# Gate loop and feed-forward kernel: rows of w3 and w_out fetched as one tile, four at a time, and a two-word conversion with one three-operand instruction fewer

## The chip, the cores and the metric

The kernel runs on one core of a Trainium2 chip. The metric is device time in microseconds, the median over executions; lower is better. Each run executed the kernel before on the same chip in alternation. A ratio is the mean time of one kernel's fast runs over the mean of the other's of the same rounds, so it is not quite the ratio of the medians that are quoted.

In the tables of the profile PE is TensorE (PEld its weight loads), DVE is VectorE, ACT is ScalarE, POOL is GpSimd, and SPq is the queue of SyncE, which issues all transfers here.

## The reference

```python
B, H, S, D = 4, 8, 768, 48
scale = np.minimum(mag, 0.999) / (mag + 1e-06)        # mag = |a_re + i a_im|
for t in range(S):                                    # complex recurrence, decay by the gate
    S_re, S_im = (ar * S_re - ai * S_im + kv), (ar * S_im + ai * S_re)
    y[:, :, t] = np.einsum('bhd,bhde->bhe', q[:, :, t], S_re)
# ... then, on x = y as (3072, 384):
a = x @ w1; b = x @ w2                                # 384 x 1024 each
h = a * b @ w3                                        # 1024 x 1024
return h @ w_out                                      # 1024 x 384
```

The four weight matrices arrive as 64-bit floats. The core has no such type, so the kernel reads them as pairs of 32-bit words and puts 32-bit floats together from them: it shifts the high word left by three, puts its top two bits (the sign and one of the exponent; "the sign" below) back, and adds the top three bits of the low word, rounded ("the carry" below). Since h is linear in w3, it multiplies w3 by w_out once and uses the product.

## The kernel before

The first stage does two things side by side. It takes w3 and w_out row by row (eight rows of 128 by 1024 and 128 by 384), converts them, and multiplies them into eight sums. And it computes the gates of the first unit (half of the 768 time steps of one batch entry; there are eight units), a chain that alternates between ScalarE and VectorE. Each piece of weights takes one of three raw buffers:

```python
    def convert(dst, src, halves):
        r, m = dst.shape[1:]
        raw = cv["raw"].tile([P, r, m, 2], I32, tag="raw", name="raw")          # pool of 3
        nc.sync.dma_start(out=raw.rearrange("p r m w -> p r (m w)"), in_=src)
        lo, hi = raw[:, :, :, 0], raw[:, :, :, 1]
        low = cv["low"].tile([P, r, m], I32, tag="low", name="low")
        b = dst.bitcast(I32)
        if halves:          # w3: carry into the low half of each word, sign into the high half
            ...             # two ScalarE instructions
            nc.vector.tensor_scalar(out=b, in0=hi, scalar1=3, scalar2=None, op0=OP.logical_shift_left)
        else:               # w_out, w1, w2
            nc.scalar.activation(out=low, in_=lo.bitcast(U32), func=AF.Copy, scale=2.0 ** -29)
            nc.vector.tensor_scalar(out=b, in0=hi, scalar1=3, scalar2=0x3FFFFFFF, ...)
            nc.vector.scalar_tensor_tensor(out=b, in0=hi, scalar=-0x40000000, in1=b, ...)
        nc.vector.tensor_tensor(out=b, in0=b, in1=low, op=OP.add)
```
```python
        row_work(0, 4)                       # row 0 in four parts
        load_gates(0)
        take_qk(0)
        steps = gates(0, True)
        for f in range(KF):                  # KF = 8 rows
            if f:
                row_work(f)                  # loads and converts row f
            if f == 2:
                load_qkv(0)
            if f >= KF - 2:
                continue
            for j in range(KF):
                fuse(f, j)                   # line 924, the product on TensorE
            for _ in range(2):
                next(steps, None)            # two steps of the gates
```

KL and QL, the tiles into which K and Q are moved at the end of the gates, stand empty until then.

Of the kernel before, what the change touches and what calls it, by code (L numbers as in the profile page):

```python
# [10 lines left out]
FP = mybir.dt.float32  # L11
I32 = mybir.dt.int32
U32 = mybir.dt.uint32
U16 = mybir.dt.uint16
BF = mybir.dt.bfloat16
AF = mybir.ActivationFunctionType
OP = mybir.AluOpType
# [357 lines left out]
def kernel(  # L375
# [36 lines left out]
    nc = tc.nc  # L412
    B, H, D, S = qt.shape
    P = 128
# [3 lines left out]
    FF = w1.shape[1]  # L418
    KD = DM // P
    DG = P // H  # L420
    KF = FF // P
    WB = 2 * P
# [13 lines left out]
    w1s = weights_pool.tile([P, FF // WB, KD, WB], FP, name="w1s")  # L436
    w2s = weights_pool.tile([P, FF // WB, KD, WB], FP, name="w2s")
# [7 lines left out]
    one = fast.enter_context(tc.tile_pool(name="one", bufs=1))  # L445
# [36 lines left out]
    def load_rows(dst, src, u, which=range(KD), queue=nc.sync):  # L482
        b, h = divmod(u, 2)
        for i, f in enumerate(which):
            queue.dma_start(out=dst[:, i, 0:TT], in_=src[b, :, DG * f:DG * (f + 1), h * TT:(h + 1) * TT].rearrange(
                "h d s -> d h s"))

    def load_gates(u):
        g = g_t.setdefault(u, {})
        for n, src in (("re", art), ("im", ait)):  # L490
            g[n] = one.tile([P, KD, TT], FP, tag=n, name=n)
            load_rows(g[n], src, u)

    def take_qk(u):
        g = g_t.setdefault(u, {})
        g["q"] = gate_pool[u % 2].tile([P, KD, TT], FP, tag="q", name="q")
        g["k"] = gate_pool[u % 2].tile([P, KD, TT + 1], FP, tag="k", name="k")

    def load_qkv(u):
        b, h = divmod(u, 2)  # L500
        if "q" not in g_t.get(u, {}):
            take_qk(u)
        g = g_t[u]
        load_rows(g["k"], kt, u)
        load_rows(g["q"], qt, u)


        vr = one.tile([P, UC, DM], FP, tag="vr", name="vr")
        nc.sync.dma_start(out=vr, in_=v[b, h * TT:(h + 1) * TT].rearrange("(c p) e -> p c e", p=C))
        g["vr"] = vr  # L510
# [306 lines left out]

    cv = {}

    def convert(dst, src, halves):  # L820
        r, m = dst.shape[1:]
        raw = cv["raw"].tile([P, r, m, 2], I32, tag="raw", name="raw")
        nc.sync.dma_start(out=raw.rearrange("p r m w -> p r (m w)"), in_=src)
        lo, hi = raw[:, :, :, 0], raw[:, :, :, 1]
        low = cv["low"].tile([P, r, m], I32, tag="low", name="low")
        b = dst.bitcast(I32)
        if halves:
            ends = low.rearrange("p r m -> p (r m)")
            nc.scalar.activation(out=ends.bitcast(U16)[:, 0::2].rearrange("p (r m) -> p r m", r=r), in_=lo.bitcast(U32),
                                 func=AF.Copy, scale=2.0 ** -29)  # L830
            nc.scalar.activation(out=ends.bitcast(BF)[:, 1::2].rearrange("p (r m) -> p r m", r=r), in_=hi.bitcast(FP),
                                 func=AF.Sign)
            nc.vector.tensor_scalar(out=b, in0=hi, scalar1=3, scalar2=None, op0=OP.logical_shift_left)
        else:
            nc.scalar.activation(out=low, in_=lo.bitcast(U32), func=AF.Copy, scale=2.0 ** -29)
            nc.vector.tensor_scalar(out=b, in0=hi, scalar1=3, scalar2=0x3FFFFFFF, op0=OP.logical_shift_left,
                                    op1=OP.bitwise_and)
            nc.vector.scalar_tensor_tensor(out=b, in0=hi, scalar=-0x40000000, in1=b, op0=OP.bitwise_and,
                                           op1=OP.bitwise_or)
        nc.vector.tensor_tensor(out=b, in0=b, in1=low, op=OP.add)  # L840

    def load_weight(dst, src, halves=False):
        if src.dtype == FP:
            nc.sync.dma_start(out=dst, in_=src)
        else:
            convert(dst, src, halves)

    def words(src):
        return (src if src.dtype == FP else src.bitcast(I32)).rearrange("(i p) m -> p i m", p=P)
# [34 lines left out]
    w3_t = {}  # L884

    def rounding():

        stack = ExitStack()
        for n, k in (("raw", 3), ("low", 2)):
            cv[n] = stack.enter_context(tc.tile_pool(name=n, bufs=k))  # L890
        return stack

    def columns(src, j0, j1):
        n = 1 if src.dtype == FP else 2
        return words(src)[:, :, n * j0:n * j1]

    def w12_work():
        return [lambda d=d, w=w, n=n: load_weight(d[:, n], columns(w, n * WB, (n + 1) * WB))
                for n in range(FF // WB) for d, w in ((w1s, w1), (w2s, w2))]

    def row_work(f, parts=1):

        if f == 0:
            w3_t["wo"] = one.tile([P, KF, DM], FP, tag="ab", name="wo_s")
        w3_t[f] = two.tile([P, FF], FP, tag="xT", name="w3s")

        def some(n):
            step = FF // parts
            load_weight(w3_t[f][:, n * step:(n + 1) * step].rearrange("p (i m) -> p i m", i=1),
                        columns(w3t, n * step, (n + 1) * step)[:, f:f + 1], True)  # L910
        some(0)
        load_weight(w3_t["wo"][:, f:f + 1], words(wo)[:, f:f + 1])
        for n in range(1, parts):
            some(n)


    sums = []
# [51 lines left out]
    def ffn(u, parts=1):  # L969
        if u == 0:  # L970
            return [lambda j=j: ffn_ab(u, j) for j in range(KF)] + [p for t in range(UC) for p in ffn_out(u, t, parts)]
        last = ffn_out(u, UC - 1)[0]
        return [lambda j=j: ffn_ab(u, j) for j in range(KF)] + [lambda: (out_sums(u), last())] + out_pair(u)
# [17 lines left out]
    with tc.manual_schedule(engines={mybir.EngineType.PE}):  # L991

        phase = rounding()
        row_work(0, 4)
        load_gates(0)
        take_qk(0)
        steps = gates(0, True)
        for f in range(KF):
            if f:
                row_work(f)  # L1000
            if f == 2:
                load_qkv(0)
            if f >= KF - 2:
                continue
            for j in range(KF):
                fuse(f, j)
            for _ in range(2):
                next(steps, None)
        work = w12_work()
        for f in work[:2]:  # L1010
            f()
        for _ in steps:
            pass
        for f in range(KF - 2, KF):
            for j in range(KF // 2):
                fuse(f, j)
        fill = [lambda f=f, j=j: [fuse(f, j + x) for x in range(2)] for f in range(KF - 2, KF) for j in range(KF // 2, KF, 2)]
        load_gates(1)
        steps = gates(1, False)
        take_qk(1)  # L1020
        rest = ffn(0, 2)
        work = work[2:]
        for i, p in enumerate(pieces(0)):
            for f in p:
                f()
            if i in (1, 3, 6, 9):
                fill.pop(0)()
            if i == 0:
                for f in work[:2]:
                    f()  # L1030
                load_qkv(1)
            if i >= 2:
                next(steps)
            if i in (5, 7):
                work[2 + (i == 7)]()
        for i, f in enumerate(rest[:HEAD]):
            f()
            if i < 2:
                work[4 + i]()
            if i == 2:  # L1040
                phase.close()
            if i < 6:
                next(steps)
            if i == KF - 1:
                for _ in steps:
                    pass
        late = fast.enter_context(tc.tile_pool(name="late", bufs=1))
        look = check_weights(fast.enter_context(tc.tile_pool(name="looks", bufs=2)))
        out_weights()
        for u in range(1, NU):  # L1050
            steps = gates(u + 1, False) if u + 1 < NU else iter(())
            unit(u, steps, rest[HEAD:] if u == 1 else ffn(u - 1), look if u > 1 else iter(()), AHEAD[u])
            for _ in steps:
                pass
        for _ in look:
            pass
        judge()
        for f in ffn(NU - 1):
            f()
# [41 lines left out]
```

## Time and profile before

| | before |
|---|---|
| median of the time | 581.5 us (579.2 to 582.9) |
| span of the profiled execution | 581.6 us |
| TensorE idle | 34.8 us, of it 18.4 waiting for converted rows |
| row 7 ready for TensorE | 60.64 us |
| first feed-forward matmul | 89.12 us |

Read it so: TensorE is busy for 94 per cent of the span, so nearly all that can be won lies in its idle time. Idle time on other engines matters only where TensorE waits for them. The lines that show the waits are in the prediction.

### The profile page before, as it was taken

The numbers are of one execution on the slowest core, as the hardware profiler recorded it, in microseconds if no ns is written. First come the engines' busy times: TensorE is split into PE (matmuls) and PEld (weight loads), VectorE is DVE, ScalarE is ACT, GpSimd is POOL, SyncE is SP. The second block draws the span as 40 slices with busy tenths as digits, with TensorE's granted clock in tenths as the row PEclk, the third lists the DMA queues.
The fourth block names the chain that finished last, engine by engine and source line by source line (L and its number), as shares of the span: only waits on it lengthen the run. The fifth ranks groups of instructions, "written<-read, shape, count | busy, mean of one in ns | idle before, by whom it ended". The sixth has DMA issues, their size and how long they took to land.

```text
span 581.6 us, 9282 instructions
## 1 busy us (share of the span) xinstructions
PE 546.8 (94%) x3682; PEld 388.0 (67%) x3682; DVE 341.3 (59%) x507; ACT 348.5 (60%) x576; POOL 3.5 (1%) x9
## 2 busy tenths in 40 slices
PE   4579898999999999999989999999989999999995
PEld 2345585567656885679556975687557966697564
DVE  6898588965771477535952677444852787241121
ACT  5898648464764589628973799459973945111100
POOL 2000000000000000000000000000000000000000
PEclk9779999999999999999999999999999999999999
DMA  7877999376056335973486336935484103300001
GB/s 233 278 289 274 228 308 300 105 156 170 26 157 146 96 106 178 244 194 116 140 229 162 112 121 189 240 97 162 127 188 117 57 27 87 89 3 29 0 4 43
DMA packets 46340, 84.74 MB, mean 146 GB/s; under 512 B 4688, under 2 KB 36176, under 8 KB 45392
## 3 DMA queue, kind: packets, MB, share of 16 engines
q1 hardware_dynamic: 46288, 84.06, 51.1%
q8 instruction: 31, 0.51, 0.4%
q14 instruction: 21, 0.17, 0.1%
HBM read 60.42 MB, written 4.72 MB: 112 GB/s over the span
## 4 chain that ended last, share of the span: by engine, by line
PE 64%; ACT 13%; DMA 11%; DVE 8%; issue 3%; SPq 0%; ACTq 0%; DVEq 0%
PE m L723 34%; PE p L768 9%; PE o L803 7%; DMA raw<-in_w_dram 5%; PE kv L703 4%; PE sc L665 4%; PE y L692 3%; DMA look<-in_w_dram 3%; PE tp L653 2%; DMA vr<-in_v_dram 2%; ACT gZ L544 2%; ACT gR L544 2%; ACT re L544 1%; DVE gA L576 1%; DVE gZ L600 1%
## 5 line engine op out<-in xcount | busy, mean ns | idle before, releaser
L723 PE MATMUL m<-xT,w1s 128*128 128x384 f32 x384 | 135.4, 489 | 5.5 <-ACT xT L694 3.1
L723 PE MATMUL m<-xT,w2s 128*128 128x384 f32 x384 | 134.3, 486 | 0.0
L723 PEld LDWEIGHTS m<-xT,w2s 128*128 128x128 f32 x384 | 73.0, 190 | 50.9
L723 PEld LDWEIGHTS m<-xT,w1s 128*128 128x128 f32 x384 | 71.0, 190 | 51.8 <-ACT xT L694 4.3
L729 DVE TENSOR_TENSOR ab<-m,a 128x384 f32<-128x384 f32 x64 | 35.5, 556 | 82.7 <-PE m L723 74.4
L924 PE MATMUL f<-wo_s,w3s 128*128 128x384 f32 x128 | 51.0, 559 | 18.4 <-DVE wo_s L840 18.4
L728 ACT COPY a<-m 128x384 f32<-128x384 f32 x64 | 30.4, 476 | 49.7 <-PE m L723 49.6
L655 ACT COPY KT<-tp 128x384 f32<-128x384 f32 x40 | 33.7, 853 | 35.3 <-PE tp L653 35.2
L803 PE MATMUL o<-w3o,ab 128*128 128x384 f32 x160 | 53.8, 487 | 0.0
L924 PEld LDWEIGHTS f<-wo_s,w3s 128*128 128x128 f32 x128 | 27.5, 220 | 39.4 <-DVE wo_s L840 20.3
L665 PE MATMUL sc<-QL,KL 96*128 96x128 f32 x384 | 47.2, 276 | 1.9 <-DMA QL<-q 1.4
L665 PEld LDWEIGHTS sc<-QL,KL 96*128 96x128 f32 x384 | 45.7, 192 | 3.0 <-DMA QL<-q 1.5
L803 PEld LDWEIGHTS o<-w3o,ab 128*128 128x128 f32 x160 | 29.6, 190 | 18.9 <-issue 0.4
L692 PE MATMUL y<-A,V 128*32 128x128 f32 x768 | 39.3, 275 | 0.0
L667 DVE COPY_PREDICATED A<-causal,sc 128x512 f32<-128x512 int32 x48 | 34.0, 738 | 5.8 <-PE sc L665 5.5
L710 DVE TENSOR_TENSOR T<-kv,T 96x512 f32<-96x512 f32 x16 | 11.0, 687 | 42.4 <-PE kv L703 42.4
L692 PEld LDWEIGHTS y<-A,V 128*32 128x32 f32 x768 | 32.9, 109 | 3.6 <-issue 1.4
L692 PE MATMUL y<-QL,T 96*32 96x128 f32 x640 | 34.6, 272 | 0.0
L768 PE MATMUL p<-To,So 128*128 128x192 f32 x168 | 31.5, 331 | 0.5 <-DVE U L756 0.5
L544 ACT ACTIVATE re<-gZ 128x1152 int32<-128x1152 f32 (+3 forms) x20 | 19.2, 970 | 20.8 <-DVE gZ L600 16.4
L692 PEld LDWEIGHTS y<-QL,T 96*32 96x32 f32 x640 | 31.3, 110 | 0.0
L703 PE MATMUL kv<-V,KT 128*96 128x64 f32 x320 | 30.0, 246 | 0.9 <-ACT KT L655 0.9
(116 smaller groups left out, 760.8 us busy)
## 6 DMA issues: line engine op xcount, KB each, us to landing
look<-in_w_dram SPq DMA_DIRECT2D x28, 512.0 KB, 4.0
raw<-in_w_dram SPq DMA_DIRECT2D x7, 1024.0 KB, 8.0
raw<-in_w_dram SPq DMA_DIRECT2D x8, 768.0 KB, 7.0
KL<-gR SPq DMA_DIRECT2D x24, 192.5 KB, 3.4
KL<-k SPq DMA_DIRECT2D x24, 192.5 KB, 4.2
re<-in_a_re_dram SPq DMA_DIRECT2D x24, 192.0 KB, 5.4
im<-in_a_im_dram SPq DMA_DIRECT2D x24, 192.0 KB, 3.3
k<-in_k_dram SPq DMA_DIRECT2D x24, 192.0 KB, 3.7
```

What stands on the lines that cost most here:

```text
L544: chain(nc.scalar.activation(**kw))
L655: nc.scalar.copy(out=KT_t[u, c][:, :, :, x].rearrange("p h d f -> p f d h"), in_=tp.rearrange("p f (d h) -> p f d h", h=H))
L665: nc.tensor.matmul(out=sc[:, j], lhsT=KL[:, x * n + j, w], rhs=QL[:, x * n + j, w], start=True, stop=True)
L667: nc.vector.copy_predicated(out=A[:, x * n:(x + 1) * n], data=sc, mask=causal.rearrange("p (h t) -> p h t", h=1).to_broadcast([P, n, C]))
L692: nc.tensor.matmul(out=o, lhsT=a, rhs=b, start=s0, stop=s1)
L703: nc.tensor.matmul(out=kv[:, hd], lhsT=KT[:, hd].rearrange("p d x f -> p (d x f)"), rhs=V[:, hd], start=True, stop=True)
L723: nc.tensor.matmul(out=m, lhsT=w[:, j * P // WB, f, j * P % WB:j * P % WB + P], rhs=xT_t[u][:, f], start=(f == 0), stop=(f == KD - 1))
L728: copied[:] = [nc.scalar.copy(out=a, in_=got[0])]
L729: nc.vector.tensor_tensor(out=ab_t[u][:, j], in0=got[1], in1=a, op=OP.mult)
L768: nc.tensor.matmul(out=m[p], lhsT=a[:, f], rhs=b[:, f], start=(f == 0), stop=(f == KH - 1))
L803: nc.tensor.matmul(out=m, lhsT=ab_t[u][:, f, t * P:(t + 1) * P], rhs=w3o[:, f], start=(f == 0), stop=(f == KF - 1))
L924: nc.tensor.matmul(out=sums[j], lhsT=w3_t[f][:, j * P:(j + 1) * P], rhs=w3_t["wo"][:, f], start=(f == 0), stop=(f == KF - 1))
```

## The change

The intent is to have more rows on their way, and less work for VectorE in the conversion. A row's words of w3 and w_out come in one tile of 12 KB per partition. Four such tiles are in flight: two in the raw pool and two in the room of KL and QL. w1 and w2 also share a tile. And in the conversion of w_out, w1 and w2 the sign, masked out by a plain tensor_scalar, is put into the low word before ScalarE writes the carry into its lower 16 bits.

```diff
+    def fetch(srcs, early=None):
+        pool, tag = (one, early) if early else (cv["raw"], "raw")
+        raw = pool.tile([P, 6 * WB * 2], I32, tag=tag, name="raw")
+        ...            # one transfer for each source, side by side in the tile
@@ load_weight
+        if not halves:
+            nc.vector.tensor_scalar(out=low, in0=hi, scalar1=-0x40000000, scalar2=None, op0=OP.bitwise_and)
+        nc.scalar.activation(out=<low halves of low>, in_=lo.bitcast(U32), func=AF.Copy, scale=2.0 ** -29)
         else:
-            nc.scalar.activation(out=low, in_=lo.bitcast(U32), func=AF.Copy, scale=2.0 ** -29)
             nc.vector.tensor_scalar(out=b, in0=hi, scalar1=3, scalar2=0x3FFFFFFF, ...)
-            nc.vector.scalar_tensor_tensor(out=b, in0=hi, scalar=-0x40000000, in1=b, ...)
         nc.vector.tensor_tensor(out=b, in0=b, in1=low, op=OP.add)
@@
-        for n, k in (("raw", 3), ("low", 2)):
+        for n, k in (("raw", 2), ("low", 2)):
@@ row_load
+        w3_t[f] = fetch([...], {0: "KL", 1: "QL"}.get(f % 4))
@@
-        row_work(0, 4)
+        row_load(0, 4)
         load_gates(0)
+        row_load(1); row_load(2); row_load(3)
         ...
         for f in range(KF):
-            if f: row_work(f)
-            if f == 2: load_qkv(0)
+            row_work(f)
+            if f == 0: load_qkv(0)
+            if f + 4 < KF: row_load(f + 4)
```

More of the change, by code (lines that the diff above doesn't have):

```diff
@@ L818, with load_weight @@
     cv = {}
-    def convert(dst, src, halves):
+    def fetch(srcs, early=None):
+        if srcs[0].dtype == FP:
+            return srcs
+        pool, tag = (one, early) if early else (cv["raw"], "raw")
+        raw = pool.tile([P, 6 * WB * 2], I32, tag=tag, name="raw")
+        got, n = [], 0
+        for src in srcs:
+            r, m = src.shape[1:]
+            t = raw[:, n:n + r * m].rearrange("p (r m) -> p r m", r=r)
+            nc.sync.dma_start(out=t, in_=src)
+            got.append(t.rearrange("p r (m w) -> p r m w", w=2))
+            n += r * m
+        return got
+    def load_weight(dst, src, halves=False):
+        if src.dtype == FP:
+            nc.sync.dma_start(out=dst, in_=src)
+            return
+        lo, hi = src[:, :, :, 0], src[:, :, :, 1]
         r, m = dst.shape[1:]
-        raw = cv["raw"].tile([P, r, m, 2], I32, tag="raw", name="raw")
-        nc.sync.dma_start(out=raw.rearrange("p r m w -> p r (m w)"), in_=src)
-        lo, hi = raw[:, :, :, 0], raw[:, :, :, 1]
         low = cv["low"].tile([P, r, m], I32, tag="low", name="low")
+        ends = low.rearrange("p r m -> p (r m)")
         b = dst.bitcast(I32)
+        if not halves:
+            nc.vector.tensor_scalar(out=low, in0=hi, scalar1=-0x40000000, scalar2=None, op0=OP.bitwise_and)
+        nc.scalar.activation(out=ends.bitcast(U16)[:, 0::2].rearrange("p (r m) -> p r m", r=r), in_=lo.bitcast(U32),
+                             func=AF.Copy, scale=2.0 ** -29)
         if halves:
-            ends = low.rearrange("p r m -> p (r m)")
-            nc.scalar.activation(out=ends.bitcast(U16)[:, 0::2].rearrange("p (r m) -> p r m", r=r), in_=lo.bitcast(U32),
-                                 func=AF.Copy, scale=2.0 ** -29)
             nc.scalar.activation(out=ends.bitcast(BF)[:, 1::2].rearrange("p (r m) -> p r m", r=r), in_=hi.bitcast(FP),
@@ L834, in convert @@
         else:
-            nc.scalar.activation(out=low, in_=lo.bitcast(U32), func=AF.Copy, scale=2.0 ** -29)
             nc.vector.tensor_scalar(out=b, in0=hi, scalar1=3, scalar2=0x3FFFFFFF, op0=OP.logical_shift_left,
                                     op1=OP.bitwise_and)
-            nc.vector.scalar_tensor_tensor(out=b, in0=hi, scalar=-0x40000000, in1=b, op0=OP.bitwise_and,
-                                           op1=OP.bitwise_or)
         nc.vector.tensor_tensor(out=b, in0=b, in1=low, op=OP.add)
-    def load_weight(dst, src, halves=False):
-        if src.dtype == FP:
-            nc.sync.dma_start(out=dst, in_=src)
-        else:
-            convert(dst, src, halves)
     def words(src):
@@ L897, in w12_work, with block, row_load, row_work @@
     def w12_work():
-        return [lambda d=d, w=w, n=n: load_weight(d[:, n], columns(w, n * WB, (n + 1) * WB))
-                for n in range(FF // WB) for d, w in ((w1s, w1), (w2s, w2))]
-    def row_work(f, parts=1):
+        got = {}
+        def block(n, i):
+            if i == 0:
+                got[n] = fetch([columns(w, n * WB, (n + 1) * WB) for w in (w1, w2)])
+            load_weight((w1s, w2s)[i][:, n], got[n][i])
+        return [lambda n=n, i=i: block(n, i) for n in range(FF // WB) for i in range(2)]
+    def row_load(f, parts=1):
+        step = FF // parts
+        w3_t[f] = fetch([columns(w3t, 0, step)[:, f:f + 1], words(wo)[:, f:f + 1]] +
+                        [columns(w3t, n * step, (n + 1) * step)[:, f:f + 1] for n in range(1, parts)],
+                        {0: "KL", 1: "QL"}.get(f % 4))
+    def row_work(f):
         if f == 0:
             w3_t["wo"] = one.tile([P, KF, DM], FP, tag="ab", name="wo_s")
+        got = w3_t[f]
         w3_t[f] = two.tile([P, FF], FP, tag="xT", name="w3s")
-        def some(n):
-            step = FF // parts
-            load_weight(w3_t[f][:, n * step:(n + 1) * step].rearrange("p (i m) -> p i m", i=1),
-                        columns(w3t, n * step, (n + 1) * step)[:, f:f + 1], True)
-        some(0)
-        load_weight(w3_t["wo"][:, f:f + 1], words(wo)[:, f:f + 1])
-        for n in range(1, parts):
-            some(n)
+        step = FF // (len(got) - 1)
+        for n, src in enumerate(got[0:1] + got[2:]):
+            load_weight(w3_t[f][:, n * step:(n + 1) * step].rearrange("p (i m) -> p i m", i=1), src, True)
+            if n == 0:
+                load_weight(w3_t["wo"][:, f:f + 1], got[1])
     sums = []
@@ L993 @@
         phase = rounding()
-        row_work(0, 4)
+        row_load(0, 4)
         load_gates(0)
+        row_load(1)
+        row_load(2)
+        row_load(3)
         take_qk(0)
@@ L998 @@
         for f in range(KF):
-            if f:
-                row_work(f)
-            if f == 2:
+            row_work(f)
+            if f == 0:
                 load_qkv(0)
+            if f + 4 < KF:
+                row_load(f + 4)
             if f >= KF - 2:
```

## The prediction

> **What bounds the kernel now.** I read the page's forty slices first, then the waits of TensorE and of the DMA queue, then the timelines of the first 66 us, and last the groups of the conversion lines.
>
> ```profile
> PE   4579898999999999999989999999989999999995
> DVE  6898588965771477535952677444852787241121
> ACT  5898648464764589628973799459973945111100
> PEclk9779999999999999999999999999999999999999
> DMA  7877999376056335973486336935484103300001
> ```
>
> A slice is 14.5 us. From slice 5 on TensorE is at 8 or 9 tenths to the end. Only the first four slices have room, and there VectorE, ScalarE and the DMA engines are all near full. In slices 2 and 3 the clock is below full as well.
>
> ```profile
> PE f L924 <- DVE wo_s L840: 18.4, 4, 7.3
> PE m L723 <- ACT xT L694: 3.1, 3, 1.8
> PE sc L665 <- DMA QL<-q: 1.4, 1, 1.4
> ```
>
> These are waits of TensorE over the whole span: total, times, longest. 18.4 us in four gaps is the wait for a converted row of w3 and w_out before the product w3·w_out (line 924). The span is 581.6 us and TensorE busy 546.8 us, so 34.8 us are idle, and over half of that is this wait. Its four places, from TensorE's timeline (start, length, idle before):
>
> ```profile
> 7.28 8.30 PE L924 MATMUL f<-wo_s,w3s 128*128 128x384 f32 x16 [7.28 <-DVE wo_s L840]
> 21.79 13.04 PE L924 MATMUL f<-wo_s,w3s 128*128 128x384 f32 x32 [6.21 <-DVE wo_s L840]
> 38.63 20.89 PE L924 MATMUL f<-wo_s,w3s 128*128 128x384 f32 x56 [3.81 <-DVE wo_s L840]
> 60.64 2.85 PE L924 MATMUL f<-wo_s,w3s 128*128 128x384 f32 x8 [1.12 <-DVE wo_s L840]
> ```
>
> A row is 16 matmul records, so this is row 0; rows 1 and 2; rows 3, 4, 5 and half of 6; half of 7. The rest of the product fills later places. Two gaps are long enough to cost speed after them too (window; busy and count of PE, PEld, DVE, ACT, POOL; clock; DMA share; GB/s):
>
> ```profile
> 20.00:24.00 4.00, 2.21 (x4) 1.29 (x5) 3.92 (x7) 3.97 (x8) 0.00 (x0) 0.50 0.65 198
> 40.00:44.00 4.00, 4.00 (x8) 2.14 (x7) 4.00 (x10) 2.98 (x6) 0.00 (x0) 0.52 0.83 301
> 48.00:52.00 4.00, 4.00 (x14) 2.34 (x13) 4.00 (x9) 3.97 (x7) 0.00 (x0) 1.00 0.82 260
> ```
>
> At clock 1.00 weight loads follow each other by about 0.32 us, after the gaps by 0.64 us (22.59, 23.23, 23.87). About 8 records in the second stretch, 8 in the third and 10 at the very start run slow: 0.32 us lost on each, 8.3 us in all.
>
> Why rows are late, from the waits of the DMA queue and its timeline:
>
> ```profile
> SPq L823 <- DVE w3s L833: 28.4, 8, 7.1
> ```
> ```profile
> 11.68 0.33 SPq L823 DMA_DIRECT2D raw<-in_w_dram  x1
> 20.03 0.33 SPq L823 DMA_DIRECT2D raw<-in_w_out_dram  x1
> 20.41 1.83 SPq L485 DMA_DIRECT2D k<-in_k_dram  x3
> 53.47 0.60 SPq L630 DMA_DIRECT2D KL<-k  x1
> 58.39 0.37 SPq L823 DMA_DIRECT2D raw<-in_w_dram  x1
> 58.81 0.57 SPq L630 DMA_DIRECT2D QL<-gA  x1
> ```
>
> With three raw buffers, and w3 and w_out taking one each, one and a half rows are in flight. The queue stands 8 us at 11.68 and holds back k behind it; at 53.47 it stands again and holds back the move of Q into QL. But rows are late for a second reason: from 20 to 40 us VectorE is busy 9.93 of each 10 us. So two things bind the stage, buffers and VectorE, with ScalarE (9.21 and 9.62 of 10) just behind.
>
> **What the Trainium skill says.** "Perfetto Trace Analysis", Optimization Strategy: a gap that repeats on the engine that should be saturated can mean too little SBUF for the next tile. The 28.4 us over eight waits agree. "DMA: Bandwidth & Descriptors", Anatomy of one DMA: a semaphore wait is taken on the issuing sequencer, before dispatch. The lines at 11.68 and 53.47 agree: later transfers stand behind one that waits. "TensorE: Matmul & The Clock Gate", Part 1: after an idle window of about 3.4 us the array drops to half clock, and it needs about as long a busy one to come back. The trace agrees: the gaps of 6.21 and 3.81 us end at clock 0.50, and about 5 us of matmuls run so. "VectorE: DVE Perf Modes", The perf-mode tier table: a 32-bit tensor_scalar runs at two elements a cycle, a tensor_tensor at one. The page doesn't list the three-operand form; the trace puts it with the slow ones (0.96 against 0.56 us, below).
>
> **The change, part by part.**
>
> (1) Cheaper conversion of w_out, w1 and w2. The sign, masked out by a tensor_scalar, goes into the low word before ScalarE writes the carry into its lower half; the scalar_tensor_tensor goes away.
>
> ```profile
> L838 DVE SCALAR_TENSOR_TENSOR wo_s<-raw,wo_s 128x384 int32<-128x384 int32 x8 | 4.4, 550 | 0.1
> L836 DVE TENSOR_SCALAR wo_s<-raw 128x384 int32<-128x384 int32 x8 | 2.8, 353 | 0.3 <-DMA raw<-in_w_out_dram 0.3
> L838 DVE SCALAR_TENSOR_TENSOR w1s<-raw,w1s 128x768 int32<-128x768 int32 x4 | 3.8, 957 | 0.1
> L836 DVE TENSOR_SCALAR w1s<-raw 128x768 int32<-128x768 int32 x4 | 2.3, 564 | 1.2 <-DMA raw<-in_w_dram 1.2
> ```
>
> The new instruction has the form of line 836, so I give it its time. w_out: 8 × (0.550 − 0.353) = 1.6 us. w1 and w2: 8 × about 0.40 = 3.2 us, of which 2 × 0.40 just after row 7 and 6 × 0.40 = 2.4 us between 75 and 115 us. All of it is VectorE, 4.8 us. ScalarE keeps its count and sizes. It adds one order: ScalarE's carry now follows a VectorE instruction, a possible short stall.
>
> (2) One tile for a row, four in flight. The queue no longer waits for a buffer in the first 10 us: row 0, the gates and rows 1 to 3 are issued back to back. Is there DMA room? 110, 272, 265 and 315 GB/s in the first four 4-us windows give 3.85 MB by 16 us, at a share of 0.80 to 0.92 from 4 us on. Row 0 (1.44 MB), the gates (1.18) and row 1 (1.44) are 4.06 MB, so row 1 can't land before about 15.5 to 16 us; today its halves are used at 17.46 and 18.41. The gain for row 1 is 1.5 to 2.5 us. Later rows come well ahead of VectorE: rows 2 and 3 at about 20 and 25 us at 300 GB/s.
>
> (3) What VectorE then allows. From 17.46 to 60.60 us, when row 7 is converted, it idles only 0.25 + 0.68 + 1.87 = 2.8 us, so it has 40.3 us of work there. Less 7 × 0.2 = 1.4 us this is 38.9 us. Starting at 16 us and without a wait it is done at 54.9 us; I add 1.5 us for waits on ScalarE, and get 56.4 us. That is 4.2 us sooner, the main term.
>
> (4) TensorE. Rows then come about every (56.4 − 19) / 6.5 = 5.8 us, and a row takes 16 × 0.32 = 5.1 us at full clock. The long gaps shrink to under a microsecond each, too short to lose the clock. That wins much inside the stage, but its end is still set by row 7: the product ends at 56.4 + 2.9 = 59.3 us instead of 63.5. The 4.2 us stand; the clock is not added to them.
>
> (5) After that. TensorE is nearly full, so what it starts earlier ends earlier. Two waits may shrink: 1.75 us before the first feed-forward matmul at 89.12, where ScalarE stood for V until 87.94 behind moves and weight loads, and 1.4 us for QL of the next unit, which hangs on VectorE being full from 94 to 120 us, where 2.4 us go away. I count 2.2 of these 3.2 us.
>
> (6) K and Q. The moved K and Q need tiles that raw rows 4 and 5 hold. Those are converted by about 45 us; the first move is issued at 47.8 today. No cost. k and q of unit 0 now stand behind rows 1 to 3 and land near 27 to 29 us; q is used at 27.23 today. Cost 0 to 1 us, I take 0.4, as gates and rows share VectorE and rows can go first.
>
> Sum: 4.2 + 2.2 − 0.4 = 6.0, and I add 0.9 (a guess) for the moves of unit 0, no longer held from 53 to 58 us, and so for what is queued behind them. 580.9 − 6.9 = 574.0.
>
> **Rivals.** *Buffers were the only bound.* Then all of 6.21 + 3.81 + 1.12 us and 5.1 us of the half clock go: up to 16 us, 565. Against it: VectorE at 9.93 of 10; it would need 38.9 us of work in some 32. *VectorE and ScalarE alone bind.* Then only (1) counts, 2 to 4 us, 577 to 579. Against it: the 2.8 us of idle and the late start at 17.46. *A new wait takes the gain.* k and q late, or QL and KL taken by rows, or w1 and w2 (now one shared tile of two buffers) late; 580 to 584. For it: DMA share above 1.0 from 64 to 92 us, so anything moved into that time is paid for. Against it: the loads move earlier, away from there.
>
> **Range and chances.** Term (3) may be 2.5 to 8 us, (5) 0 to 3.2, (6) up to −2. This gives 568.5 to 579.5. A gain over 2% needs 11.6 us or more; that takes nearly the first rival: 0.14. A loss over 2% would need a long new stall: 0.03. Within 2%: 0.83.
>
> **What would show it.** Right: no queue wait for a raw buffer before 10 us; the wait of line 924 falls from 18.4 to about 10 to 12 us, 7 of them at the start; clock 1.00 from 30 us on; row 7's last add near 56 us; line 838's sites at 0.35 and 0.56 us; first feed-forward matmul near 83 us. Wrong: rows ready by 50 us (VectorE reordered, rival one); VectorE waiting for q or ScalarE for VectorE's new instruction by microseconds; moves waiting for rows 4 and 5.

## The result

The changed kernel took 573.85 us (573.55 to 574.82, four runs) against 581.51 us, a ratio of 0.9875 with an interval of 0.984 to 0.991. Two repeats, in later batches on chips 11 and 8, gave 0.9881 and 0.9869. The prediction was 574.0 us.

| | before | after |
|---|---|---|
| median of the time | 581.5 us | 573.85 us |
| TensorE idle in the profiled execution | 34.8 us | 27.5 us |
| of it waiting for rows | 18.4 us | 15.7 us |
| row 7 ready for TensorE | 60.64 us | 55.74 us |
| first feed-forward matmul | 89.12 us | 83.53 us |
| span | 581.6 us | 571.8 us |

The forty slices of the kernel after, in tenths, now 14.3 us each:

```profile
PE   4688999999999999999999999999999999999995
DVE  6899489946852567446852786255743696241121
ACT  6998668538572798549972999279954845111110
PEclk9799999999999999999999999999999999999998
DMA  8994997393273355954584427845482104200001
```

In slices 2 and 3 the DMA engines are at 9 tenths and in slice 4 at 4. The rows have all been fetched by then. The first four slices of VectorE and ScalarE stay near full. The queue no longer waits for a buffer at the start: rows 1 to 3 are issued between 6.99 and 11.2 us, where row 2 took from 11.68 to 20.36 us before. The last of them, row 3:

```profile
10.12 0.33 SPq L830 DMA_DIRECT2D raw<-in_w_dram  x1
10.83 0.33 SPq L830 DMA_DIRECT2D raw<-in_w_out_dram  x1
```

TensorE's timeline of the row product (start, length, idle before):

```profile
7.21 7.84 PE L941 MATMUL f<-wo_s,w3s 128*128 128x384 f32 x16 [7.21 <-DVE wo_s L855]
19.91 18.64 PE L941 MATMUL f<-wo_s,w3s 128*128 128x384 f32 x48 [4.86 <-DVE wo_s L855]
40.68 13.53 PE L941 MATMUL f<-wo_s,w3s 128*128 128x384 f32 x40 [2.13 <-DVE wo_s L855]
55.74 2.85 PE L941 MATMUL f<-wo_s,w3s 128*128 128x384 f32 x8 [1.53 <-DVE wo_s L855]
```

The shape is that of before: a start at 7.2 us, two gaps inside, one before row 7. Row 1 comes 1.9 us sooner. Row 7 comes 4.9 us sooner, and it is the one that counts. The waits of TensorE over the whole span (total, times, longest):

```profile
PE f L941 <- DVE wo_s L855: 15.7, 4, 7.2
...
PE m L723 <- ACT xT L694: 1.0, 2, 0.6
PE m L723 <- ACT a L728: 0.6, 1, 0.6
```

The wait of 1.4 us for QL is gone, that for xT fell from 3.1 to 1.0 us, and that for a (line 728) from 2.4 to 0.6 us. From the first feed-forward matmul to the end it took 492.5 us before and 488.3 us after. But the profiled execution of before was a long one for that kernel (583.4 us, median 581.5), so part of these 4.2 us is a difference between executions. The traces of the experiments below help: with the old arithmetic and the new buffers this part took 490.6 us, in the twelve traces with the new arithmetic 487.6 to 489.6 us. By the medians 7.7 us went. By this pair of traces some 5.6 of them lie before the first feed-forward matmul, and the rest, about 2 us, after it.

What binds the first stage now? From the windows and the groups of the kernel after (groups: busy us, mean ns, idle before):

```profile
16.00:55.00 39.00, 32.07 (x88) 17.86 (x88) 35.85 (x67) 37.02 (x56) 0.00 (x0) 0.91 0.77 277
44.00:48.00 4.00, 4.00 (x14) 2.39 (x13) 4.00 (x8) 3.97 (x8) 0.00 (x0) 1.00 0.01 4
L855 DVE CUSTOM_DVE_ANT_0 w3s<-w3s,low 128x2048 uint16<-128x2048 uint16 x7 | 8.6, 1222 | 3.0 <-ACT low L849 3.0
L846 ACT ACTIVATE low<-raw 128x384 uint16<-128x384 uint32 x8 | 4.9, 617 | 0.8 <-DVE low L845 0.8
```

The first line is the stretch from 16 to 55 us, with PE, PEld, DVE, ACT and POOL in this order: of 39 us VectorE is busy 35.85 and ScalarE 37.02. The second has DMA at a share of 0.01. In the third VectorE stood 3.0 us for ScalarE's sign of w3. So after the change ScalarE is as near its limit as VectorE, and from 14 to 60 us neither of them waits for a transfer. The fourth shows a cost that the prediction left out: ScalarE's carry for 384 columns took 536 ns when it wrote whole words, and takes 617 ns now that it writes every second half word. For 768 columns it is 938 and 1085 ns.

Where do the 4.9 us of row 7 come from? VectorE either works or waits, so the stretch from its first instruction of row 1 to its last of row 7 can be added up. Before it is 17.46 to 60.59 us with 2.8 us of waits and 40.3 us of work, after it 15.29 to 55.68 us with 3.05 us of waits and 37.35 us of work. So VectorE began row 1 2.2 us sooner, did 3.0 us less, and waited 0.25 us more. The arithmetic explains 7 × 0.2 = 1.4 us of the work. The rest is a change of order. Three of the twelve products at the end of the gates (K and Q times sine and cosine, lines 634 to 639), 0.55 us each, now come behind row 7; before, all twelve came ahead of it. Row 7's last instruction, and two of the three:

```profile
55.13 0.55 DVE L855 CUSTOM_DVE_ANT_0 wo_s<-wo_s,low 128x768 uint16<-128x768 uint16 x1
56.54 0.55 DVE L635 TENSOR_TENSOR k<-k,gZ 128x384 f32<-128x384 f32 x1
59.29 0.55 DVE L639 TENSOR_TENSOR q<-q,gZ 128x384 f32<-128x384 f32 x1
```

The program fixes only TensorE's order (`tc.manual_schedule(engines={PE})`); VectorE's and ScalarE's are chosen when the kernel is built, and VectorE's is the same in all three traces of the changed kernel. No wait of TensorE for what the three products write shows in the trace.

### The profile page after: what moved, and what is told of

Read it like the earlier page. It is cut to its first block, busy times and chain, and to the rows that moved or that the text cites. A ratio compares the mean times of both kernels' runs of the same rounds, so it can differ in the third digit from the quotient of the medians.

```text
span 571.8 us, 9285 instructions
## 1 busy us (share of the span) xinstructions
PE 544.3 (95%) x3682; PEld 386.6 (68%) x3682; DVE 335.6 (59%) x507; ACT 348.8 (61%) x576; POOL 3.5 (1%) x9
## 4 chain that ended last, share of the span: by engine, by line
PE 64%; ACT 13%; DVE 11%; DMA 6%; issue 4%; SPq 1%; ACTq 0%; DVEq 0%
PE m L723 36%; PE p L768 9%; PE o L803 6%; PE sc L665 4%; PE y L692 4%; PE kv L703 3%; ACT gZ L544 2%; DMA re<-in_a_re_dram 2%; ACT re L544 2%; PE tp L653 2%; ACT gR L544 2%; DMA QL<-gA 1%; DVE gZ L600 1%; ACT gA L544 1%; DMA look<-in_w_dram 1%
## 5 line engine op out<-in xcount | busy, mean ns | idle before, releaser
L941 PE MATMUL f<-wo_s,w3s 128*128 128x384 f32 x128 | 48.7, 537 | 15.8 <-DVE wo_s L855 15.7
L941 PEld LDWEIGHTS f<-wo_s,w3s 128*128 128x128 f32 x128 | 26.2, 211 | 35.8 <-DVE wo_s L855 18.4
L692 PEld LDWEIGHTS y<-A,V 128*32 128x32 f32 x768 | 32.9, 109 | 3.4 <-issue 1.1
```

Source lines behind the costliest of these rows:

```text
L692: nc.tensor.matmul(out=o, lhsT=a, rhs=b, start=s0, stop=s1)
L941: nc.tensor.matmul(out=sums[j], lhsT=w3_t[f][:, j * P:(j + 1) * P], rhs=w3_t["wo"][:, f], start=(f == 0), stop=(f == KF - 1))
```

## The experiments

The theory going in: buffers and VectorE's work bind the first stage together, and the gain comes from both parts of the change. The rivals: only buffers, only VectorE, or ScalarE. All runs gave correct results.

| kernel | median us | ratio to before (95%) |
|---|---|---|
| after, first repeat | 574.54 | 0.9881 (0.986 to 0.9903) |
| buffers only | 576.59 | 0.9907 (0.9887 to 0.9927) |
| arithmetic only | 579.99 | 0.9975 (0.9951 to 1.0) |
| two rows in flight | 576.97 | 0.9914 (0.989 to 0.9939) |
| more VectorE work | 575.14 | 0.9903 (0.9876 to 0.993) |
| more ScalarE work | 576.57 | 0.9924 (0.9897 to 0.9952) |
| k, q, v loaded later | 575.13 | 0.9893 (0.9866 to 0.9919) |
| v spread by GpSimd | 574.09 | 0.9874 (0.9848 to 0.9901) |
| after, second repeat | 573.76 | 0.9869 (0.9845 to 0.9894) |
| three rows changed over | 574.88 | 0.9887 (0.9861 to 0.9912) |
| seven rows changed over | 574.28 | 0.9876 (0.985 to 0.9902) |
| seven, and q on GpSimd | 577.11 | 0.9927 (0.9902 to 0.9952) |

The intervals are wide because the kernel before scatters by 3.6 to 5.0 us in a batch; the changed kernel's own runs lie within 573.1 to 575.4 us in all three batches. The first four rows are one batch, the next four a second, the last four a third, each on a chip of its own. The second had no run of the changed kernel. For it I take the ratio 0.9875, which is the mean of the three that there are (0.9875, 0.9881, 0.9869); 0.001 is 0.58 us. A difference found in this way is uncertain by more than a microsecond where it rests on the ratios; for the two runs with added work the difference of the plain means, against 574.1 us for all 15 executions of the changed kernel, is given beside it.

One rival runs through all of this and was not tested: the order of work. Most edits below also change the order on VectorE and ScalarE. A sign of it is how many of the twelve last gate products come behind row 7: three in all three traces of the changed kernel and with v on GpSimd; none before, with the arithmetic only, with two rows in flight and with more ScalarE work; one with k, q, v later and with q on GpSimd; two with three rows changed over; four with the buffers only; five with more VectorE work and with seven rows changed over. The times show what each edit does with the order that comes with it. What the order alone is worth, no run shows.

### The changed kernel again

> The changed kernel once more, beside the others of this batch. 573 to 575 us, ratio to before 0.985 to 0.990. It is the yardstick for the three below; no theory hangs on it.

574.54 us. Its first stage was not quite the same as in the first profile: gaps of 5.29 and 2.64 us, and after the second the clock was below full once more, at 0.67 from 40 to 44 us. Row 7 was ready at 55.68 us all the same, and the span was 571.3 us. What TensorE does inside the stage varies between executions, and it doesn't set the end.

### Buffers only

```diff
-        if not halves:
-            nc.vector.tensor_scalar(out=low, in0=hi, scalar1=-0x40000000, scalar2=None, op0=OP.bitwise_and)
         else:
+            nc.scalar.activation(out=low, in_=lo.bitcast(U32), func=AF.Copy, scale=2.0 ** -29)
             nc.vector.tensor_scalar(out=b, in0=hi, scalar1=3, scalar2=0x3FFFFFFF, ...)
+            nc.vector.scalar_tensor_tensor(out=b, in0=hi, scalar=-0x40000000, in1=b, ...)
```

> The changed kernel with the old arithmetic for w_out, w1 and w2 (scalar_tensor_tensor back). VectorE gets 8 x 0.2 us more in the first stage and 8 x 0.4 us more for w1 and w2. Theory of the prediction (both parts count): 1.5 to 3.5 us over the changed kernel, about 576 us, ratio 0.990 to 0.994. Rival, buffers are all that counts: within 0.7 us of the changed kernel. Rival, ScalarE is now the bound (its old form is 0.54 instead of 0.62 us on 384 columns and 0.94 instead of 1.09 us on 768): as fast as the changed kernel or up to 1 us faster.

576.59 us: 5.2 us faster than before by the means (576.51 against 581.72), 1.9 us slower than the changed kernel of the same batch (574.57). This is where the first theory put it; both rivals fall. Its waits of TensorE:

```profile
PE f L942 <- DVE wo_s L856: 15.8, 4, 7.2
PE m L723 <- ACT xT L694: 2.3, 3, 1.2
PE tp L653 <- DVE gR L616: 1.6, 1, 1.6
PE sc L665 <- DMA QL<-q: 1.4, 1, 1.4
```

The wait of 1.4 us for QL is back as it was before, and row 7 starts only 0.3 us later than in the changed kernel (56.06). Here VectorE had 1.4 us more to do for rows 1 to 7, but four products instead of three came behind row 7. So much of what the arithmetic is worth on top of the buffers comes after row 7: the first feed-forward matmul came 1.0 us later (84.55 us), and what follows it took 2.3 us longer.

### Arithmetic only

```diff
 # in the kernel before
+        if not halves:
+            nc.vector.tensor_scalar(out=low, in0=hi, scalar1=-0x40000000, scalar2=None, op0=OP.bitwise_and)
+        nc.scalar.activation(out=<low halves of low>, in_=lo.bitcast(U32), ...)
-            nc.scalar.activation(out=low, in_=lo.bitcast(U32), ...)
-            nc.vector.scalar_tensor_tensor(...)
```

> The kernel before with the new arithmetic and its old buffers. Theory (VectorE and buffers bind together): 1 to 3 us faster than before, ratio 0.995 to 0.998. Rival, VectorE alone binds: nearly the whole gain, 576 us or less. Rival, buffers alone: no change, within 0.7 us, as rows are late whatever VectorE does; slower if ScalarE's waits on VectorE add up.

579.99 us, 1.4 us faster by the means (580.30 against 581.72); the interval just reaches 1.0, so the rival of no change is made unlikely and not excluded by this run. Row 7 started at 60.07 us, 0.6 us sooner than before: VectorE had 1.4 us less to do for rows 1 to 7, with all gate products ahead of row 7, but began row 1 0.2 us later and waited 0.6 us more. The queue waited for buffers as before. There was no wait for QL. The parts add up: 5.2 us (buffers, means) and 1.4 us make 6.6, and together they gave 7.15 us in this batch (581.72 − 574.57); the 0.5 us between is within the scatter.

### Two rows in flight

```diff
-        w3_t[f] = fetch([...], {0: "KL", 1: "QL"}.get(f % 4))
+        w3_t[f] = fetch([...], None)
-        row_load(1); row_load(2); row_load(3)
+        row_load(1)
-            if f + 4 < KF: row_load(f + 4)
+            if f + 2 < KF: row_load(f + 2)
```

> The changed kernel with one tile for a row but only two of them, both in the raw pool, none in the place of moved K and Q. Theory that 1.5 to 2 rows in flight starve the converters: 2 to 4 us slower than the changed kernel (576 to 578), with the queue waiting for buffers again. Rival, two whole rows are enough because VectorE and ScalarE set the pace and four only look good: within 1 us of the changed kernel.

576.97 us, 2.3 us slower than the changed kernel by the means (576.85 and 574.57). The queue waited again:

```profile
SPq L830 <- DVE wo_s L853: 14.2, 4, 4.0
```

Row 7 was ready at 58.10 us, 2.4 us later: VectorE began row 1 1.4 us later, and all twelve gate products came ahead of row 7. So the four rows, and the room of KL and QL with them, are needed for about a third of the gain, by sooner rows and by the order that comes with them.

### More VectorE work

```diff
-            nc.vector.tensor_scalar(out=b, in0=hi, scalar1=3, scalar2=None, op0=OP.logical_shift_left)
+            for _ in range(2 if m == FF else 1):
+                nc.vector.tensor_scalar(out=b, in0=hi, scalar1=3, scalar2=None, op0=OP.logical_shift_left)
```

> The changed kernel with the shift of w3 done twice in rows 1 to 7: 7 x 0.60 us = 4.2 us more VectorE work in the first stage, nothing else. Theory (VectorE sets the pace after the change): 3 to 4.2 us slower than the changed kernel, about 577.5 us, row 7 converted near 59 us. Rival (ScalarE sets the pace, VectorE stood 3.1 us waiting for it between 16 and 55 us): 0 to 1.5 us slower. Rival (arrival of rows): no change.

575.14 us, ratio 0.9903, which is 0.0028 or 1.6 us over the changed kernel (1.3 by the plain means). The row 7 product:

```profile
57.65 2.85 PE L942 MATMUL f<-wo_s,w3s 128*128 128x384 f32 x8 [1.23 <-DVE w3s L856]
```

It began 1.9 us later, not 4.2. The other 2.3 us: VectorE waited 0.8 us less, began row 1 0.4 us sooner, and had two more gate products behind row 7 (1.1 us). So "nothing else" in the expectation does not hold; the order changed too. The forecast for VectorE setting the pace, 3 to 4.2 us, is missed clearly; the rival's, 0 to 1.5 us, is met or missed by 0.1 us.

### More ScalarE work

```diff
+        if halves and m == FF:      # the first half of the columns twice
+            nc.scalar.activation(out=<low halves of low, first half>, in_=lo[:, :, 0:m // 2].bitcast(U32), ...)
```

> The changed kernel with half of ScalarE's carry of w3 done twice in rows 1 to 7: 7 x about 0.61 us = 4.3 us more ScalarE work in the first stage, nothing else. If VectorE alone sets the pace: 0 to 1.5 us slower than the changed kernel. If ScalarE sets it, or both do in turn: 2.5 to 4.3 us slower, about 577.5 us. Arrival of rows: no change.

576.57 us, ratio 0.9924, 0.0049 or 2.8 us over the changed kernel (2.6 by the plain means).

```profile
58.90 2.85 PE L944 MATMUL f<-wo_s,w3s 128*128 128x384 f32 x8 [1.65 <-DVE wo_s L858]
```

Row 7 began 3.2 us later. VectorE waited 2.0 us more, and all twelve gate products came ahead of row 7 (1.5 us more work there), less 0.4 us for a sooner start. So ScalarE's work counts: of 4.3 us added, some two thirds reach the end, where of VectorE's 4.2 us it was under a half. VectorE alone as the limit falls with this. That both engines limit the stage in turn fits the two runs; that ScalarE counts more than VectorE is not shown, as half of the delay of row 7 here came with the order.

### k, q and v loaded later

```diff
-            if f == 0:
+            if f == 2:
                 load_qkv(0)
```

> The changed kernel with k, q and v of unit 0 loaded after row 2, where they were, and so behind rows 4 to 6 in the queue's order. If their new place was needed: VectorE or ScalarE waits for q, k or v by 2 us or more, and it is 1 to 4 us slower. If there is slack: within 0.7 us.

575.13 us, ratio 0.9893, 1.0 us over the changed kernel if 0.9875 is taken for it; the intervals overlap. It falls between the two expectations. The profiled execution, the slowest of its six, had five waits of TensorE for rows in place of four, and row 7 came at 57.36 us; from 14 to 60 us neither VectorE nor ScalarE waited for q, k or v. The new place of the load is no cost, and perhaps a small gain.

### v spread by GpSimd

```diff
-            nc.scalar.copy(out=V[:, :, :, i, e0:e0 + D], in_=vr[:, :, :, i])
+            nc.gpsimd.tensor_copy(out=V[:, :, :, i, e0:e0 + D], in_=vr[:, :, :, i])
```

> The changed kernel with the spreading of v done by GpSimd, which is 1 per cent busy, in place of ScalarE: ScalarE is rid of 1.2 us in the first stage and of standing for v of the next unit. If ScalarE bounds the first stage together with VectorE: 0.5 to 1.5 us faster than the changed kernel. If VectorE alone does: within 0.5 us. It could be slower if the copies on GpSimd take long or hold VectorE up.

574.09 us, ratio 0.9874: no change. In the profiled execution, the slowest of the six (575.19 us), ScalarE's load from 16 to 55 us fell to 34.15 us, but VectorE then stood 2.6 us for TensorE to release a w3 tile, TensorE having waited 4.2 us before rows 1 and 4 each, and row 7 came at 58.27 us. VectorE's order is that of the changed kernel here, and still the relief is not a clean one. GpSimd spread v from 28.77 to 30.5 us, and VectorE's two adds of row 3 in that time took 1.02 and 1.68 us, where they take 0.56 and 1.23 us in the changed kernel. So ScalarE was relieved by 1.2 us and VectorE lost 0.9 us, as the expectation had allowed for. Whether relief of ScalarE alone would gain anything is not shown.

### The arithmetics changed over, in three and in seven rows

```diff
-            load_weight(<w3 row>, src, True)
+            load_weight(<w3 row>, src, f not in (2, 4, 6))        # second kernel: 1 to 7
-                load_weight(w3_t["wo"][:, f:f + 1], got[1])
+                load_weight(w3_t["wo"][:, f:f + 1], got[1], f in (2, 4, 6))
```

The batch had the changed kernel in it as a yardstick. (The second of the texts reckons with 1.3 and 2.4 us for the two runs with added work, near the plain means above.)

> The changed kernel once more, as the yardstick of this batch: 573 to 575 us, ratio 0.986 to 0.990.

573.76 us, as expected.

> The changed kernel with the two arithmetics changed over in rows 2, 4 and 6: w3 by the mask on VectorE, w_out by the sign on ScalarE (the row's product stays halved, so the result is right on these inputs; the guard for large values does not cover w_out then). In each such row ScalarE does about 0.8 us less and VectorE 0.33 us more. By the slopes of the two runs with added work (VectorE 4.2 us more cost about 1.3 us, ScalarE 4.3 us more about 2.4 us): 3 x 0.8 x 0.56 - 3 x 0.33 x 0.3 = 1.0 us faster than the changed kernel. If VectorE alone sets the pace: 0.3 to 1 us slower.

574.88 us, 1.0 us slower by the means (574.73 and 573.75) where 1.0 us faster was expected.

> The same changeover in rows 1 to 7: ScalarE 5.4 us less, VectorE 2.3 us more in the first stage. If ScalarE bounds most: 1.5 to 3 us faster than the changed kernel, about 572 us. If VectorE takes over as the bound: 0 to 1 us faster. If VectorE alone was the bound: 1.5 to 2.3 us slower.

574.28 us, 0.4 us slower by the means, where 0 to 3 us faster was expected. Its stretch from 16 to 55 us:

```profile
16.00:55.00 39.00, 32.32 (x89) 18.16 (x89) 37.55 (x66) 31.97 (x55) 0.00 (x0) 0.91 0.78 280
```

ScalarE fell from 37.02 to 31.97 us, and VectorE rose from 35.85 to 37.55 us and waited for ScalarE no more. The limit has passed to VectorE. In this trace the first stage did get shorter: VectorE ended row 7 at 54.86 us (55.68 in the changed kernel), with five gate products behind it, and the first feed-forward matmul came at 82.84 us (83.53). What follows took 489.6 us, against 488.3 us, and so nothing was left. So my expectations, the first made from the slopes of the two runs with added work, were wrong: what work added to an engine costs does not tell what the same work taken away gains, while the other engine is just as full and the order changes. With three rows ScalarE stood 3.4 us for VectorE in this stretch and VectorE 2.1 us for ScalarE, so neither ran free of the other.

### Seven rows changed over, and q on GpSimd

```diff
-            tt(out=q[:, s], in0=q[:, s], in1=A[:, s], op=OP.mult)
+            (nc.gpsimd.tensor_tensor if u == 0 else tt)(out=q[:, s], in0=q[:, s], in1=A[:, s], op=OP.mult)
```

> The run with seven rows changed over, and the three products of q and the decay of unit 0 on GpSimd in place of VectorE: VectorE 1.4 us less. If VectorE is the bound after the changeover: 0.5 to 1.4 us faster than that run. If it is not, or GpSimd takes long or holds VectorE up: no change or slower.

577.11 us, 2.9 us slower than the seven rows alone (means 577.09 and 574.15).

```profile
L588 POOL TENSOR_TENSOR q<-q,gA 128x384 f32<-128x384 f32 x3 | 5.4, 1829 | 23.4 <-DMA q<-in_q_dram 23.4
```

A product of 384 columns took 1829 ns on GpSimd (1308 to 2202, and spans on GpSimd are rough), where VectorE's took 0.55 us. And while GpSimd worked, from 27.47 to 32.9 us, VectorE's own instructions were longer: 1.15 and 2.02 us for the two adds of row 3 (0.56 and 1.22 us in the seven rows alone), 1.82 us for two instructions of the gates (1.02). That is 2.2 us lost, against three products of 0.55 us taken off. ScalarE stood 4.0 us for VectorE's gate steps, and row 4 was late by 3.6 us against the seven rows alone (43.67 and 40.04). No version that beats the changed kernel was found.

## Why the prediction was right, and where its steps were not

It was right in the time (574.0 and 573.85 us). Its two causes, buffers and arithmetic, hold, as each part alone and both together were run. But its steps 3, 4 and 6 were wrong in part, errors cancelled inside step 3 and in the sum, and one cost was left out. Of the signs that it named, these came: no wait of the queue for a raw buffer before 10 us, row 7's last add at 55.68 us, the new instruction at 0.355 and 0.55 us, the first feed-forward matmul at 83.53 us. Two did not: TensorE's wait for rows fell to 15.7 us only, and the clock was at 1.00 from 30 us on in the first trace but not in the repeats (0.67 and 0.75 from 40 to 44 us). And one sign of being wrong did come: ScalarE stood for VectorE's new instruction (line 845) by microseconds, 0.8 us in all at w_out and 4.1 us at w1 and w2. Before, it stood 0.1 and 4.3 us at these places, for transfers and for VectorE, so no cost of it is seen.

**Step 1, the arithmetic.** Right. The new tensor_scalar took 355 and 551 ns, as its twin of line 836 had. Taken alone the arithmetic gave 1.4 us, and taken out of the changed kernel it cost 1.9 us. Left out was ScalarE: I wrote that it keeps its count and sizes. The count holds, but the strided write costs 8 × (617 − 536) + 8 × (1085 − 938) ns = 1.8 us more.

**Step 2, arrival.** Nearly right. Row 1 came a little sooner than the 15.5 to 16 us: VectorE began it at 15.29 us and ScalarE at 15.60 us, neither having waited for it. The DMA share was 1.0 and more from 4 to 40 us, where I had counted with 0.80 to 0.92, and then nothing was left to fetch: 0.01 from 44 to 48 us. So the later rows did come ahead of their use.

**Step 3, what VectorE allows.** Right in size, and partly by luck: row 7's last add ended at 55.68 us where 56.4 was predicted. VectorE began row 1 0.7 us sooner than I had put it. It waited 3.05 us and not 1.5, all of it for ScalarE's sign of w3: the waits that I wanted gone are not fewer than the 2.8 us of before, they are for another engine (before, 1.9 of them were for TensorE). And it had 37.35 us of work and not 38.9, because three gate products went behind row 7, of which I had not thought. The last two cancel. As to the mechanism, I gave VectorE's work as the limit. The runs with added work show that it is not the only one: 4.2 us more on VectorE cost 1.6 us, and 4.3 us more on ScalarE 2.8 us. That the limit is the pair, with their work interleaved, fits all runs, but as the order changed with almost every edit it is argued and not shown. No run relieved VectorE or ScalarE alone and changed nothing else.

**Step 4, TensorE inside the stage.** Wrong in its first half. The gaps did not shrink to under a microsecond; they were 4.86, 2.13 and 1.53 us, the wait came to 15.7 us and not to 10 to 12, and after the first gap the clock was again at 0.50 from 20 to 24 us. The rows are not evenly spaced, as I had worked it out: VectorE did gate steps alone from 30.5 to 37.3 us. The second half held: the end of the stage is set by row 7. In the 13 traces that have a gap before row 7 the first feed-forward matmul comes 27.3 to 28.9 us after it, and in the first repeat other gaps inside the stage left row 7 where it was. The rival that added the gaps and the clock up to 16 us fell with this.

**Step 5, after the stage.** Right. The wait before the first feed-forward matmul fell from 1.75 to 0.45 us, and the 1.4 us for QL went away; it came back when the old arithmetic was put back. I had counted 2.2 us, and 2.7 were seen in this pair of profiles. The wait for a, 1.8 us shorter, I had not counted. The traces of buffers only and of arithmetic only don't have these 1.8 us either, so they may belong to the long execution that was profiled before.

**Step 6, K and Q.** Right that there is no cost: no wait for scores on QL or KL is left. Wrong in the guess of 0.9 us that the queue would no longer hold the moves up. It still does, now behind the fetch of the first w1 and w2 tile, which waits for row 6's tile:

```profile
29.41 0.43 SPq L830 DMA_DIRECT2D raw<-in_w_out_dram  x1
50.09 0.91 SPq L830 DMA_DIRECT2D raw<-in_w_dram  x2
51.04 0.63 SPq L630 DMA_DIRECT2D KL<-gR  x1
```

The part of K for the first move was ready at 42.6 us, the queue issued nothing from 29.8 to 50.1 us, and the DMA engines were all but idle from 44 to 52 us before running full to 96 us. Whether moving earlier would gain anything was not tried.

**The sum.** Main term 4.2 predicted and 4.9 measured, after the stage 2.2 and 2.7 by these two waits, a cost of 0.4 and a gain of 0.9 not seen. I predicted a gain of 6.9 us, and by the medians it was 7.7. That the time agrees to 0.2 us is partly luck: the errors cancel, and I started from 580.9 us, the median of the kernel before at that time, where the batch of the result gave 581.5.

## What to carry to other kernels

When the engine that should be full waits for data, ask both what holds the transfers and what holds the conversion of what has landed: here more buffers gave 5.2 us of 7.15, and cheaper arithmetic the rest. A look at where the last piece becomes ready tells more than the sum of the gaps; the gaps fell by only 2.7 us while the last row came 4.9 us sooner. When two engines work in turn and both are near full, a microsecond of work on one of them is not a microsecond of time: 4.2 us more on VectorE cost 1.6 us here, 4.3 us more on ScalarE 2.8 us, and shifting work from ScalarE to VectorE gained nothing. And where the order of work is chosen for you, look whether an edit has changed it before you put a difference down to the edit: of the 4.9 us here, 1.65 came from three instructions that went behind the last row.

## What the Trainium skill lacked or had wrong

- "ScalarE: Activation LUTs" (What ACT_TABLE_LOAD costs) gives an ACTIVATE with immediate operands 186 ns + 0.833 ns an element, for every function, fp32 and bf16 alike. For packed 32-bit data that fits (1152 elements: 1157 to 1167 ns here, 1146 by the page). For the words of 64-bit floats, read at every second place, it is more: 384 elements took 536 ns (506 by the page) and 768 took 938 ns (826). When the 16-bit results also went to every second half word it was 617, 1085 and, for 1024 elements, 1357 ns (1039). Number form and step changed together, so it is not shown which of them costs. That page says nothing on strides; another page of the skill does, but has no ScalarE time for them.
- "VectorE: DVE Perf Modes" (The perf-mode tier table) doesn't list scalar_tensor_tensor. On 768 32-bit integers it took 957 ns, against 564 ns for the tensor_scalar on the same data. The skill is not silent on it, as another of its pages has a line on its throughput, but no page has a time.
- "GPSIMD Engine Reference" (Engine selection) puts a two-input elementwise operation at about twice VectorE's time. Here, on 384 columns beside a busy VectorE, it was 1829 ns on average against 0.55 us, over three times, and VectorE's own instructions became longer meanwhile.
